# Spreading attention over the first MoE by the emitter's own clock instead of a table of unit times

## The chip, the cores and the metric

The kernel runs on one core of a Trainium2 chip. The metric is the device time of one execution in microseconds; before the change it is 749.09 us, the median of 3 runs (747.17 to 750.77). A profile was taken of one further execution.

## What is computed

Three layers, one after the other, all in float32 accuracy:

```python
scores = scale * q @ k.T          # 4 batches, 8 heads, 576 tokens, 64 wide
mask: block of 64 tokens sees itself and earlier blocks
x = softmax(scores) @ v           # then heads side by side: (4, 576, 512)

xk, xr = mixes of x[t] and x[t-1] by mu_k, mu_r        # first MoE
x = sigmoid(xr @ w_r) * (relu(xk @ w_k)**2 @ w_v)

h = gelu(x @ w_in); u, v = halves of h                  # second MoE
v = layernorm(v) * g_ln; v = w_sg @ v + b_sg            # over tokens
x = x + (u * v) @ w_out
```

The matmuls of the MoEs run on pairs: each operand is split into a rounded high part and the rest, and three products are summed (`xh*w0`, `xl*w0`, `xh*w1`). The weights come as float64 words and are put together on VectorE and ScalarE (`w_split`, lines 212 to 231).

## The kernel before

**Attention** is cut into 64 units: one head of one batch, and of its tokens the first 320 (kind LO) or the last 256 (kind HI). The list `units` runs LO of batch 0 (units 0 to 7), LO of batch 1 (8 to 15), HI of batch 0 (16 to 23), HI of batch 1 (24 to 31), and the same for batches 2 and 3 (32 to 63). A unit has three parts on PE: scores into the PSUM tiles `SA` and `SB` (`emit_S`; each tile has one buffer), transposes of the probabilities `P` into `T` (`emit_T`), and the products with V into `O` (`emit_PV`). Between them stand maxima (DVE, `stats`), exponentials (ACT, line 338), norms (DVE, line 348), copies of T (ACT `PH`, DVE `PL`), and after the products ACT `otmp` and DVE `xT`. The generator `attention` emits for step s, in this order: transposes of unit s-2, scores of unit s, products of unit s-2 (`LAG = 2`). The scores are so two units ahead of the products. Units below 16 (`DIRECT`) use plain float32 operands, with four passes in place of two in the emitter's count.

**The first MoE** runs in 8 halves of 288 tokens: (batch 0, first), (1, first), (0, second), (1, second), and the same of batches 2 and 3. A half is 240 matmuls of 288 columns: 96 with `w_k` (8 output blocks, 4 chunks of 3), 48 with `w_r`, 96 with `w_v`. It starts with `mix` (line 475), which makes `xh` and `xl` of the half in 4 chunks of two heads each: ACT `t`, DVE `t`, ACT `xh`, DVE or POOL `xl`. The last chunk needs the last head of the attention that this half reads, so half 1 needs units up to 15, half 2 up to 23, half 3 up to 31, half 4 up to 39, half 5 up to 47, half 6 up to 55 and half 7 all 64. The first two output blocks can do their chunks 0 to 2 without it (18 matmuls); the PSUM tile `M` has two buffers, so the 19th matmul is the first that must wait for the last chunk.

**Who sets the order.** `Order` (line 42) is a clock: `pe(ns)` adds what PE would need by `cost(n) = n / 2.4 + 13`, and work for the other engines is queued for a time on it. The loop at line 666 walks through `moe1()`, whose position x counts halves (x = 2.5 is the middle of half 2), and emits attention pieces while the attention time spent since unit 8, by the same `cost`, is below `target(x)`. `target` interpolates between knots: units needed at the next half, due at 0.85 of the half before it. It counts them with a table:

```python
UNIT_NS = [2000, 3120]                    # LO, HI
unit_t = [UNIT_NS[kind] for b, h, kind in units]
base = spent_a
```

At 0.85 of a half (line 674) whatever is still needed for the next half is emitted at once, without MoE between: `while done < need[i + 1]: att_piece()`. What is emitted so is then put in its final order on each engine by the compiler's scheduler. When all units are done, the attention memory is given back, the eight `w_in` tiles of the second MoE are loaded (line 209) and split.

Of the kernel before, what the change touches and what calls it, by code (L numbers as in the profile page):

```python
# [17 lines left out]
B, H, S = 4, 8, 576  # L18
# [2 lines left out]
CH0 = [0, 64, 192, 320, 448]  # L21
CHN = [64, 128, 128, 128, 128]
CHE = [64, 192, 320, 448, 576]

F64_MIN = struct.unpack("f", struct.pack("I", 896 << 20))[0]
F64_MAX = struct.unpack("f", struct.pack("I", (1151 << 20) - 1))[0]
# [15 lines left out]
class Order:  # L42
# [12 lines left out]
    def pe(self, ns):  # L55
        self.run(self.t)
        self.t += ns
# [12 lines left out]
    def run(self, t=float("inf")):  # L70
# [7 lines left out]
LO, HI = 0, 1  # L78
CHUNKS = [[0, 1, 2], [3, 4]]
# [3 lines left out]
GROUPS = [  # L83
    [
        ([(0, 0, 0), (0, 1, 64), (0, 2, 192)], 320),
        ([(1, 1, 0), (1, 2, 128), (2, 2, 256)], 384),
    ],
    [
        ([(0, 3, 0), (0, 4, 128)], 256),
        ([(1, 3, 0), (1, 4, 128), (2, 3, 256), (2, 4, 384)], 512),  # L90
        ([(3, 3, 0), (3, 4, 128), (4, 4, 256)], 384),
# [4 lines left out]
PRODS = [  # L96
    [(0, 0, 0, 0, 320), (1, 1, 0, 64, 256), (2, 1, 256, 192, 128)],
    [(0, 0, 0, 320, 256), (1, 1, 0, 320, 256), (2, 1, 256, 320, 256), (4, 2, 256, 448, 128),
     (3, 2, 0, 320, 256)],
]  # L100


DIRECT = 16
# [2 lines left out]
G = 2  # L106
X0_AT = 0.55
CONV2 = 2
UNIT_NS = [2000, 3120]


def cost(n):
    return n / 2.4 + 13
# [3 lines left out]
def fused_kernel(ctx: ExitStack, tc: tile.TileContext, first, qkv_lo, qkv_hi, mu,  # L117
# [6 lines left out]
    pe, at = order.pe, order.at  # L124
# [120 lines left out]
    units = [(b, h, kind) for p in range(0, B, 2) for kind in (LO, HI) for b in (p, p + 1) for h in range(H)]  # L245
    NU = len(units)
    loaded = set()
    raws, splits, vs, probs, trans, xt = {}, {}, {}, {}, {}, {}
# [34 lines left out]
    def split_v(n):  # L283
# [8 lines left out]
        copy(nc.scalar, V[:, 0:nj, odd, :], v)  # L292
        sub(nc.gpsimd, V[:, 0:nj, 1 - odd, :], v, V[:, 0:nj, odd, :].bitcast(F32))

    def emit_S(n):
        b, h, kind = units[n]
        order.need(("sp", n))
        Q, K, KL = splits.pop(n)
        chunks = CHUNKS[kind]
# [5 lines left out]
        if kind == HI:  # L305
            stc[4] = sb[:, 224:800]
        skc = [ka, ka, kb, ka, kb]
        P = probs[n] = pbuf[n % 2]
        pieces = {c: [(0, 288), (288, 576)] if c == 4 else [(0, CHE[c])] for c in chunks}
        pe(sum((2 if n >= DIRECT else 4) * cost(e - a) for c in chunks for a, e in pieces[c])  # L310
           + cost(64) * (n >= DIRECT) * sum(c > 0 for c in chunks))
        mx, sm = smax[n % 4], ssum[n % 4]
        t0, t1 = TOKENS[kind]
        nb = atile([128, 5], F32, "nb", 4)
        rr = atile([128, 5], F32, "rr", 4)
        for c in chunks:
            q0, m, e, st = CH0[c] - TOKENS[kind][0], CHN[c], CHE[c], stc[c]
            for k0, k1 in pieces[c]:
                o = st[0:m, k0:k1]
                if n < DIRECT:  # L320
                    mm(o, Q[:, q0:q0 + m], K[:, k0:k1], start=True, stop=True)
                    continue
                mm(o, Q[:, q0:q0 + m], K[:, k0:k1], start=True)
                if c > 0 and k1 == e:
                    mm(st[:, e - 64:e], mask_l, mask_r)
                mm(o, Q[:, q0:q0 + m], KL[:, k0:k1], stop=True)
# [14 lines left out]
        def norm():  # L341
# [3 lines left out]
            for c in chunks:  # L345
                m, e, o = CHN[c], CHE[c], POFF[c]

# [45 lines left out]
    def emit_PV(n):  # L393
        b, h, kind = units[n]
        order.need(("sv", n))
        V = vs.pop(n)
        odd = h % 2
        ot, ok = ptile("O", 512, 1)
        order.need(("PT", n))
        prods = PRODS[kind]  # L400
        pe(sum((2 if n >= DIRECT else 4) * cost(p[4]) for p in prods))
        t0, t1 = TOKENS[kind]
        for x, (j, u, src, q0, nq) in enumerate(prods):
            for i, part in enumerate(trans[n, u]):
                v = V[:, 64 * j:64 * j + 128] if n < DIRECT else V[:, j].rearrange("p a d -> p (a d)")
                mm(ot[:, q0 - t0:q0 - t0 + nq], v,
                   part[:, src:src + nq], start=x == 0 and i == 0, stop=x == len(prods) - 1 and i == len(trans[n, u]) - 1)
        for u in range(len(GROUPS[kind])):
            trans.pop((n, u))
        if (b, h // 2) not in xt:  # L410
            t = xt[b, h // 2] = mtile([128, S + 2], F32, "xT", XT_BUFS)
            nc.gpsimd.memset(t[:, 0:1], 0.0)
        t = xt[b, h // 2]
        r0, r1 = 64 * odd, 64 - 64 * odd
        tmp = atile([128, 320], F32, "otmp", 1)
        w = t1 - t0

        def ev1():
            copy(nc.scalar, tmp[r0:r0 + 64, 0:w], ot[r1:r1 + 64, 0:w])

        def ev2():
            nc.vector.tensor_tensor(out=t[r0:r0 + 64, 1 + t0:1 + t1], in0=ot[r0:r0 + 64, 0:w],  # L422
                                    in1=tmp[r0:r0 + 64, 0:w], op=ALU.add)

        def ev():
            copy(nc.scalar, t[r0:r0 + 64, 1 + t0:1 + t1], ot[0:64, 0:w])

        if n < DIRECT:
            at(0, ev, ok, ("x", b, kind))
            return  # L430
        at(0, ev1, ok)
        at(600, ev2, ok, ("x", b, kind))

    LAG = 2
# [176 lines left out]
    done, spent_a = 0, 0.0  # L611
# [29 lines left out]
    for i in range(1, len(halves)):  # L641
        if need[i] > knots[-1][1]:
            knots.append((i - 1 + MIX_AT, need[i]))
    unit_t = [UNIT_NS[kind] for b, h, kind in units]
    base = spent_a

    def cum(n):
        return sum(unit_t[H:n])

    all_t = cum(NU)  # L650

    def target(x):
# [316 lines left out]
```

## Time and profile before

| | |
|---|---|
| median of 3 runs | 749.09 us |
| the profiled execution, its own time | 752.42 us |
| its span, first to last instruction | 750.5 us |
| around the span | 1.9 us |
| mean granted TensorE clock | 0.973 of full speed |
| busy: PE, DVE, ACT, POOL | 93%, 71%, 58%, 44% |
| matmuls on PE | 4824 |

Stages along the span: attention alone with the first weights to 43 us, the first MoE with attention spread over it from 43 to 535 us, the second MoE from there. The view by stretches lists for each stretch the busy time of each engine, so idle time of PE is the stretch less its PE figure. The granted clock is 1.00 at 2.4 GHz and 0.50 at 1.2 GHz.

### The profile page before, as it was taken

How to read it: one execution, taken by the hardware profiler on the slowest of the kernel's cores; microseconds unless marked ns; L12 is line 12 of the kernel's file. 1: busy time of each engine (PE TensorE's matmuls, PEld its weight loads, DVE VectorE, ACT ScalarE, POOL GpSimd, SP SyncE). 2: the span in 40 equal slices, each digit the busy share in tenths (PEclk: the TensorE clock that was granted, in tenths of full speed). 3: DMA queues.
4: the chain of work that ended last, by engine and by line, in shares of the span. 5: the costliest groups of instructions: out<-in, count | busy, mean ns of one | idle time of the engine just before them, and what ended most of it. 6: DMA issues, size and time to landing. Idle time of an engine off the chain costs nothing.

```text
span 750.5 us, 13615 instructions
## 1 busy us (share of the span) xinstructions
PE 699.5 (93%) x4824; PEld 660.2 (88%) x4824; DVE 529.5 (71%) x1306; ACT 434.8 (58%) x1247; POOL 329.4 (44%) x381
## 2 busy tenths in 40 slices
PE   7878989998799899999899989988999999999998
PEld 5567869998799799999799979977999999999997
DVE  5999987778885766674885988479698736636323
ACT  4878768866795697794795788355361212122020
POOL 1437657834583386483584466134034204103021
PEclk9998999999999999999999999989999999999999
DMA  8571124223212222223222220062460120120101
GB/s 264 216 257 34 33 92 147 64 87 104 83 59 69 78 69 77 58 83 103 79 90 80 79 94 4 25 232 64 142 251 2 38 89 1 41 87 1 56 9 64
DMA packets 30724, 65.78 MB, mean 88 GB/s; under 512 B 5280, under 2 KB 16544, under 8 KB 30656
## 3 DMA queue, kind: packets, MB, share of 16 engines
q1 hardware_dynamic: 30512, 64.91, 26.5%
q8 instruction: 38, 0.62, 0.4%
q14 instruction: 30, 0.25, 0.1%
q10 hardware_dynamic: 144, 0.00, 0.0%
HBM read 55.47 MB, written 9.44 MB: 86 GB/s over the span
## 4 chain that ended last, share of the span: by engine, by line
PE 68%; DVE 14%; ACT 11%; DMA 3%; issue 3%; POOL 1%; SPq 0%; ACTq 0%; POOLq 0%; DVEq 0%
PE M L153 39%; PE O L153 14%; PE V L153 5%; PE T L370 5%; PE SB L153 3%; PE SA L153 3%; ACT P L338 2%; DVE u L222 2%; ACT PH L157 2%; DVE u L224 1%; DVE u L219 1%; DVE P L348 1%; DVE t L484 1%; DVE u L220 1%; DMA w<-w_k_dram 1%
## 5 line engine op out<-in xcount | busy, mean ns | idle before, releaser
L153 PE MATMUL M<-xh,w 128*128 128x288 f32 x768 | 178.8, 310 | 12.4 <-ACT xh L157 6.3
L153 PEld LDWEIGHTS M<-xh,w 128*128 128x128 f32 x768 | 133.0, 195 | 16.8 <-ACT R L535 7.9
L153 PE MATMUL M<-xl,w 128*128 128x288 f32 x384 | 117.2, 306 | 1.2 <-DVE xl L168 1.2
L153 PE MATMUL M<-kh,w 128*128 128x288 f32 x512 | 111.9, 300 | 3.7 <-ACT w L227 3.7
L168 DVE TENSOR_TENSOR PL<-T,PH 128x256 fp32r<-128x256 f32 (+3 forms) x128 | 68.9, 542 | 30.5 <-ACT PH L157 29.6
L153 PEld LDWEIGHTS M<-kh,w 128*128 128x128 f32 x512 | 84.7, 189 | 4.1 <-ACT w L227 4.1
L370 PE MATMUL T<-ident,P 128*128 128x128 f32 x480 | 83.5, 286 | 4.2 <-DVE P L348 2.4
L157 ACT ACTIVATE PH<-T 128x384 fp32r<-128x384 f32 (+4 forms) x144 | 68.0, 478 | 30.0 <-PE T L370 27.5
L168 POOL TENSOR_TENSOR KL<-qkv,K 128x576 fp32r<-128x576 f32 (+1 forms) x48 | 60.6, 1263 | 54.3 <-ACT K L157 40.8
L348 DVE TENSOR_SCALAR_CACHE_REDUCE P<-P,rr 64x64 f32<-64x64 f32 (+3 forms) x160 | 79.7, 536 | 1.1
L153 PEld LDWEIGHTS M<-xl,w 128*128 128x128 f32 x384 | 75.3, 196 | 2.2 <-DVE xl L168 1.8
L153 PE MATMUL M<-kl,w 128*128 128x288 f32 x256 | 76.0, 297 | 0.0
L847 POOL TENSOR_TENSOR gt<-gt,U 128x288 f32<-128x288 f32 x32 | 29.3, 920 | 100.5 <-DVE gt L843 100.4
L370 PEld LDWEIGHTS T<-ident,P 128*128 128x128 f32 x480 | 59.7, 147 | 9.1 <-issue 3.0
L168 POOL TENSOR_TENSOR xl<-t,xh 128x288 fp32r<-128x288 f32 x48 | 41.0, 855 | 49.3 <-ACT xh L157 46.8
L168 POOL TENSOR_TENSOR kl<-R,kh 128x288 fp32r<-128x288 f32 x64 | 57.8, 915 | 10.2 <-ACT kh L157 9.6
L168 POOL TENSOR_TENSOR w<-u,w 128x512 fp32r<-128x512 f32 x24 | 35.5, 1482 | 59.4 <-ACT w L227 59.4
L153 PE MATMUL O<-PH,V 128*128 128x256 f32 (+2 forms) x208 | 58.8, 294 | 3.0 <-DVE xT L422 3.0
L168 POOL TENSOR_TENSOR V<-qkv,V 128x320 fp32r<-128x320 f32 (+1 forms) x48 | 39.4, 820 | 45.2 <-ACT V L157 30.4
L153 PE MATMUL O<-PL,V 128*128 128x256 f32 (+2 forms) x208 | 56.3, 289 | 1.6 <-DVE PL L168 1.6
L153 PE MATMUL O<-gh,w 128*128 128x288 f32 x256 | 53.3, 294 | 0.0
L153 PE MATMUL M<-XHL,w 128*128 128x288 f32 x384 | 53.1, 295 | 0.0
(155 smaller groups left out, 1845.1 us busy)
## 6 DMA issues: line engine op xcount, KB each, us to landing
qkv<-qkv_hi_dram SPq DMA_DIRECT2D x32, 576.0 KB, 3.8
qkv<-qkv_lo_dram SPq DMA_DIRECT2D x16, 416.0 KB, 3.3
x2d<-x SPq DMA_DIRECT2D x32, 144.0 KB, 2.0
X<-x2d SPq DMA_DIRECT2D x4, 1152.0 KB
outT_dram<-o SPq DMA_DIRECT2D x32, 144.0 KB, 1.8
w<-w_k_dram SPq DMA_DIRECT2D x8, 512.0 KB
w<-w_v_dram SPq DMA_DIRECT2D x8, 512.0 KB, 7.6
w<-w_in_dram SPq DMA_DIRECT2D x8, 512.0 KB, 8.9
```

Of the source, the lines that this page charges most:

```text
L153: nc.tensor.matmul(out=out, lhsT=lhsT, rhs=rhs, start=start, stop=stop)
L157: nc.scalar.activation(out=out, in_=in_, func=AF.Copy)
L168: eng.tensor_tensor(out=out, in0=a, in1=b, op=ALU.subtract)
L219: nc.vector.tensor_scalar(out=v, in0=v, scalar1=F64_MIN, scalar2=F64_MAX, op0=ALU.max, op1=ALU.min)
L220: nc.vector.tensor_scalar(out=u, in0=u, scalar1=3, scalar2=0x3FFFFFFF, op0=ALU.logical_shift_left, op1=ALU.bitwise_and)
L222: nc.vector.scalar_tensor_tensor(out=u, in0=high, scalar=-0x40000000, in1=u, op0=ALU.bitwise_and, op1=ALU.bitwise_or)
L224: nc.vector.scalar_tensor_tensor(out=u, in0=low, scalar=29, in1=u, op0=ALU.logical_shift_right, op1=ALU.bitwise_or)
L338: nc.scalar.activation(out=P[0:m, po:po + e], in_=st[0:m, 0:e], func=AF.Exp, scale=0.125, bias=nb[0:m, c:c + 1], accum_out=sm[0:m, c, 0:1])
L348: nc.vector.tensor_scalar(out=P[0:m, o:o + e], in0=P[0:m, o:o + e], scalar1=rr[0:m, c:c + 1], scalar2=None, op0=ALU.mult, op1=ALU.add, acc ...
L370: nc.tensor.transpose(t[:, o:o + 128], P[:, POFF[c] + CH0[j]:POFF[c] + CH0[j] + 128], ident)
L484: nc.vector.scalar_tensor_tensor(out=t1, in0=x[:, s0 + 1:s0 + 1 + HF], scalar=mu_t[:, i, c:c + 1], in1=t1, op0=ALU.mult, op1=ALU.add)
L847: nc.gpsimd.tensor_tensor(out=gt, in0=gt, in1=U[b][:, m, fs], op=ALU.mult)
```

## The change

The table goes. `score_ns` and `out_ns` give what `emit_S`, `emit_T` and `emit_PV` hand to the clock, and the calls of `pe` in `emit_S` and `emit_PV` use them, with the same values as before. `cum(n)`, the attention time due when n units are done, sums these values: outputs of units 8 to n-1 and scores of units 8 to n+1. `base` is lowered by `cum(8)`.

```diff
--- before.py
+++ after.py
@@ -21,6 +21,7 @@
 CH0 = [0, 64, 192, 320, 448]
 CHN = [64, 128, 128, 128, 128]
 CHE = [64, 192, 320, 448, 576]
+PIECES = [[(0, 288), (288, 576)] if e == 576 else [(0, e)] for e in CHE]
 
 F64_MIN = struct.unpack("f", struct.pack("I", 896 << 20))[0]
 F64_MAX = struct.unpack("f", struct.pack("I", (1151 << 20) - 1))[0]
@@ -106,7 +107,6 @@
 G = 2
 X0_AT = 0.55
 CONV2 = 2
-UNIT_NS = [2000, 3120]
 
 
 def cost(n):
@@ -292,6 +292,15 @@
         copy(nc.scalar, V[:, 0:nj, odd, :], v)
         sub(nc.gpsimd, V[:, 0:nj, 1 - odd, :], v, V[:, 0:nj, odd, :].bitcast(F32))
 
+    def score_ns(n):
+        f, cs = (2, CHUNKS[units[n][2]]) if n >= DIRECT else (4, CHUNKS[LO])
+        return sum(f * cost(e - a) for c in cs for a, e in PIECES[c]) + cost(64) * (f == 2) * sum(c > 0 for c in cs)
+
+    def out_ns(n, trans=True):
+        kind = units[n][2]
+        return (sum((2 if n >= DIRECT else 4) * cost(p[4]) for p in PRODS[kind])
+                + trans * sum(len(g) * cost(230) for g, _ in GROUPS[kind]))
+
     def emit_S(n):
         b, h, kind = units[n]
         order.need(("sp", n))
@@ -306,16 +315,14 @@
             stc[4] = sb[:, 224:800]
         skc = [ka, ka, kb, ka, kb]
         P = probs[n] = pbuf[n % 2]
-        pieces = {c: [(0, 288), (288, 576)] if c == 4 else [(0, CHE[c])] for c in chunks}
-        pe(sum((2 if n >= DIRECT else 4) * cost(e - a) for c in chunks for a, e in pieces[c])
-           + cost(64) * (n >= DIRECT) * sum(c > 0 for c in chunks))
+        pe(score_ns(n))
         mx, sm = smax[n % 4], ssum[n % 4]
         t0, t1 = TOKENS[kind]
         nb = atile([128, 5], F32, "nb", 4)
         rr = atile([128, 5], F32, "rr", 4)
         for c in chunks:
             q0, m, e, st = CH0[c] - TOKENS[kind][0], CHN[c], CHE[c], stc[c]
-            for k0, k1 in pieces[c]:
+            for k0, k1 in PIECES[c]:
                 o = st[0:m, k0:k1]
                 if n < DIRECT:
                     mm(o, Q[:, q0:q0 + m], K[:, k0:k1], start=True, stop=True)
@@ -398,7 +405,7 @@
         ot, ok = ptile("O", 512, 1)
         order.need(("PT", n))
         prods = PRODS[kind]
-        pe(sum((2 if n >= DIRECT else 4) * cost(p[4]) for p in prods))
+        pe(out_ns(n, False))
         t0, t1 = TOKENS[kind]
         for x, (j, u, src, q0, nq) in enumerate(prods):
             for i, part in enumerate(trans[n, u]):
@@ -641,12 +648,12 @@
     for i in range(1, len(halves)):
         if need[i] > knots[-1][1]:
             knots.append((i - 1 + MIX_AT, need[i]))
-    unit_t = [UNIT_NS[kind] for b, h, kind in units]
-    base = spent_a
 
     def cum(n):
-        return sum(unit_t[H:n])
-
+
+        return sum(score_ns(u) for u in range(H, min(NU, n + LAG))) + sum(out_ns(u) for u in range(H, n))
+
+    base = spent_a - cum(H)
     all_t = cum(NU)
 
     def target(x):
```

By the code's own `cost`, an LO unit of the first 16 is 3098 ns (scores 1116, output 1982) where the table said 2000; a later LO unit is 1955 ns, a HI unit 3080 ns. The table also counted no scores of the two units ahead. By the table, then, attention falls short of what is due by a knot, the lack is carried from half to half, and the rest is emitted there in one piece: 9.3, 9.5, 8.6, 8.1, 8.5, 7.5 and 5.2 us of the emitter's clock at halves 0 to 6, and after each the next pieces come only when the target has caught up, some 0.2 to 0.5 of a half later. With the change these pieces are 0.2, 1.3, 1.4, 1.0, 0.9, 1.3 and 1.1 us, and attention is emitted from the start of each half to its end.

What the scheduler makes of it on PE, at three places. First, the start of half 5 in the kernel before: `xh_4974` is this half's input, `w_276` and `w_328` hold chunks 2 and 3 of `w_k`, `O_5196` is the output of unit 48.

```order
L153 MATMUL O_5196<-PL1_5143,V_4832 128x256
L153 MATMUL O_5196<-PH1_5142,V_4832 128x256
L153 MATMUL O_5196<-PL1_5143,V_4832 128x256
L153 MATMUL O_5196<-PH2_5158,V_4832 128x128
L370 MATMUL T_5233<-ident_60,P1_90 128x128
L153 MATMUL SA_5278<-K_4966,Q_4965 128x448
L153 MATMUL SA_5278<-mask_r_64,mask_l_63 128x64
L153 MATMUL SA_5278<-KL_4967,Q_4965 128x448
L370 MATMUL T_5233<-ident_60,P1_90 128x128
L153 MATMUL M_5044<-xh_4974,w_328 128x288
L153 MATMUL M_5060<-xh_4974,w_328 128x288
```

Behind these transposes and scores stands the first matmul with chunk 3 (`w_328`). Between the 18th MoE matmul and it stand the products of unit 47, most of those of 48, the transposes of 48 and the first of 49, and scores of units 49, 50 and 51, with no MoE between them. The products of unit 47, which chunk 3 needs, stand behind the 18th matmul too.

The same unit's products with the change (`O_4942` is the output of unit 47, `kh_4208` belongs to half 4):

```order
L153 MATMUL O_4942<-PL0_4897,V_4689 128x320
L153 MATMUL O_4942<-PH1_4903,V_4689 128x256
L377 MATMUL T_4953<-ident_60,P0_89 128x128 x2
L153 MATMUL O_4942<-PL1_4904,V_4689 128x256
L153 MATMUL O_4942<-PH1_4903,V_4689 128x128
L153 MATMUL O_4942<-PL1_4904,V_4689 128x128
L153 MATMUL M_5004<-kh_4208,w_856 128x288
L153 MATMUL M_5004<-kl_4209,w_856 128x288
L153 MATMUL M_5004<-kh_4208,w_856 128x288
L377 MATMUL T_5018<-ident_60,P0_89 128x128 x4
```

They have moved into half 4, to its 220th matmul of 240, so 20 matmuls of half 4 and the first 9 of half 5, with scores and transposes of the next units, stand between them and the first matmul that reads chunk 3.

The start of half 2 with the change (`O_2417` is the output of unit 23, the last that half 2 needs; `xh_2317` is its input):

```order
L153 MATMUL O_2417<-PL2_2375,V_2102 128x128
L153 MATMUL O_2417<-PH2_2374,V_2102 128x256
L153 MATMUL O_2417<-PL2_2375,V_2102 128x256
L377 MATMUL T_2463<-ident_60,P1_90 128x128 x4
L153 MATMUL SB_2498<-K_2310,Q_2309 128x288
L153 MATMUL SB_2498<-KL_2311,Q_2309 128x288
L153 MATMUL SB_2498<-K_2310,Q_2309 128x288
L153 MATMUL SB_2498<-mask_r_64,mask_l_63 128x64
L153 MATMUL SB_2498<-KL_2311,Q_2309 128x288
L153 MATMUL M_2432<-xh_2317,w_328 128x288
L153 MATMUL M_2471<-xh_2317,w_328 128x288
```

Here the products of unit 23 still stand behind the 18th matmul of half 2, with two score blocks between the 18th matmul and `w_328`; before, it was two score blocks in front and a third behind the 20th matmul. Elsewhere the last needed products stand, counted in the MoE matmuls of PE:

| needed by | before | with the change |
|---|---|---|
| half 1 | half 0, 192 | half 0, 190 |
| half 2 | half 2, 18 | half 2, 18 |
| half 3 | half 3, 18 | half 2, 229 |
| half 4 | half 3, 204 | half 3, 216 |
| half 5 | half 5, 18 | half 4, 219 |
| half 6 | half 6, 18 | half 5, 239 |
| half 7 | half 7, 18 | half 7, 9 |

In half 6 with the change one block of scores and most of the products of unit 56 still stand between the 18th matmul and the first with chunk 3. On DVE the order in half 0 is the same up to the last weight tile of `w_split`, but for a few instructions that change places with a neighbour, and in half 7 the splitting of `w_in` begins behind the same mix steps as before.

## Rows read from the trace of the kernel before

**Rows 1.** The page: busy time and share of the span of each engine, and of the 40 slices (18.8 us each) PE's busy tenths and the granted clock in tenths.

```profile
PE 699.5 (93%) x4824; PEld 660.2 (88%) x4824; DVE 529.5 (71%) x1306; ACT 434.8 (58%) x1247; POOL 329.4 (44%) x381
...
PE   7878989998799899999899989988999999999998
...
PEclk9998999999999999999999999989999999999999
```

**Rows 2.** Busy time in stretches (us from the span's start; busy us and instructions of PE, PEld, DVE, ACT, POOL; granted clock; DMA share and GB/s). The cuts are at matmuls counted in PE's timeline: half h of the first MoE is 240 matmuls `M<-xh`, `M<-xl`, `M<-kh` or `M<-kl`; halves 2, 3, 5, 6 and 7 begin at 171.6, 246.9, 357.9, 421.3 and 486.3, and their 25th matmul is at 202.2, 264.8, 376.9, 442.8 and 496.9.

```profile
60.00:111.50 51.50, 44.92 (x273) 39.78 (x273) 48.33 (x112) 39.39 (x117) 33.32 (x30) 0.93 0.15 46
111.50:171.60 60.10, 59.91 (x461) 59.41 (x460) 44.44 (x102) 45.68 (x131) 40.03 (x42) 1.00 0.33 107
171.60:202.20 30.60, 23.37 (x155) 21.89 (x154) 25.57 (x61) 20.85 (x61) 13.50 (x15) 0.89 0.28 87
202.20:246.90 44.70, 44.49 (x346) 43.93 (x345) 32.80 (x81) 33.66 (x100) 27.33 (x35) 1.00 0.20 62
246.90:264.80 17.90, 14.43 (x102) 13.01 (x100) 12.96 (x48) 13.46 (x46) 7.25 (x9) 0.93 0.27 81
264.80:308.50 43.70, 42.35 (x325) 41.60 (x325) 28.16 (x97) 34.64 (x116) 27.09 (x38) 0.99 0.26 79
308.50:357.90 49.40, 48.97 (x386) 48.55 (x384) 30.59 (x104) 37.09 (x122) 30.21 (x36) 1.00 0.25 79
357.90:376.90 19.00, 14.79 (x95) 13.49 (x94) 17.10 (x41) 14.98 (x43) 10.20 (x11) 0.91 0.31 102
376.90:421.30 44.40, 44.21 (x343) 43.80 (x342) 31.90 (x74) 31.37 (x93) 26.81 (x30) 1.00 0.21 66
421.30:442.80 21.50, 17.43 (x119) 16.03 (x117) 20.46 (x46) 17.47 (x51) 11.59 (x12) 0.93 0.31 99
442.80:486.30 43.50, 43.30 (x337) 42.98 (x337) 30.17 (x70) 29.80 (x85) 19.98 (x24) 1.00 0.10 33
486.30:496.90 10.60, 7.75 (x54) 7.15 (x52) 4.49 (x10) 4.39 (x10) 0.72 (x1) 0.87 0.56 173
496.90:519.00 22.10, 17.77 (x97) 15.90 (x96) 21.93 (x29) 14.92 (x37) 14.21 (x15) 0.83 0.49 168
```

**Rows 3.** The same columns, from the end of the half's 18th matmul to its 25th, of halves 2, 3, 5, 6 and 7 in this order.

```profile
181.10:202.20 21.10, 14.28 (x85) 13.04 (x84) 16.61 (x39) 15.43 (x46) 9.35 (x10) 0.84 0.28 85
250.50:264.80 14.30, 10.83 (x73) 9.41 (x71) 10.40 (x42) 10.27 (x35) 5.91 (x7) 0.91 0.28 87
361.10:376.90 15.80, 11.59 (x72) 10.32 (x71) 14.15 (x34) 12.82 (x36) 7.87 (x8) 0.89 0.34 113
426.80:442.80 16.00, 11.93 (x76) 10.57 (x74) 15.14 (x33) 13.58 (x40) 8.69 (x9) 0.90 0.29 89
490.30:496.90 6.60, 3.75 (x21) 3.15 (x20) 2.62 (x7) 3.03 (x7) 0.00 (x0) 0.80 0.63 202
```

**Rows 4.** PE's timeline after the 18th matmul of half 2: the first score matmul of three units in a row (start us, duration us, what it is, and in brackets the idle time before it and what ended it).

```profile
183.87 0.74 PE L153 MATMUL SA<-K,Q 128*128 128x448 f32 x1 [2.43 <-ACT P L338]
190.46 0.47 PE L153 MATMUL SA<-K,Q 128*128 128x448 f32 x1 [1.60 <-ACT P L338]
197.50 0.71 PE L153 MATMUL SA<-K,Q 128*128 128x448 f32 x1 [1.56 <-ACT P L338]
```

**Rows 5.** The timeline of all engines at the start of half 7: the last matmul of the last unit's output, and what follows it until PE goes on.

```profile
492.38 0.28 PE L153 MATMUL O<-PL,V 128*128 128x256 f32 x1
492.70 0.38 ACT L157 ACTIVATE otmp<-O 64x256 f32<-64x256 f32 x1 [1.29 <-PE O L153]
493.11 0.43 DVE L422 TENSOR_TENSOR xT<-O,otmp 64x256 f32<-64x256 f32 x1 [1.11 <-ACT otmp L157]
493.63 0.54 ACT L483 ACTIVATE t<-xT,um_t 128x288 f32<-128x288 f32 x1 [0.56 <-DVE xT L422]
494.20 0.52 DVE L484 SCALAR_TENSOR_TENSOR t<-xT,mu_t,t 128x288 f32<-128x288 f32 x1 [0.66 <-ACT t L483]
494.75 0.44 ACT L157 ACTIVATE xh<-t 128x288 fp32r<-128x288 f32 x1 [0.58 <-DVE t L484]
495.25 0.50 PEld L153 LDWEIGHTS M<-xh,w 128*128 128x128 f32 x2 [2.79 <-ACT xh L157]
```

**Rows 6.** Two stretches at the lower granted clock and one at the full clock that holds MoE matmuls alone (columns as in Rows 2).

```profile
371.10:374.50 3.40, 3.40 (x17) 3.40 (x18) 2.28 (x8) 3.24 (x10) 1.35 (x3) 0.54 0.09 8
439.30:442.70 3.40, 3.26 (x13) 3.12 (x14) 3.40 (x10) 3.40 (x11) 2.22 (x3) 0.55 0.23 59
407.00:410.40 3.40, 3.40 (x28) 3.40 (x27) 0.46 (x1) 0.00 (x0) 0.00 (x0) 1.00 0.63 213
```

**Rows 7.** Stretches in which attention and MoE are mixed (columns as in Rows 2): the 25th to the 145th matmul of half 6, and the fourth block of eight of halves 4 and 3.

```profile
442.80:469.60 26.80, 26.60 (x207) 26.30 (x207) 21.76 (x51) 23.29 (x69) 18.26 (x21) 1.00 0.11 36
...
324.60:331.00 6.40, 5.96 (x46) 5.58 (x45) 5.60 (x19) 6.35 (x23) 5.62 (x8) 1.00 0.32 91
276.30:283.20 6.90, 6.00 (x48) 5.77 (x46) 5.18 (x18) 6.83 (x23) 6.16 (x10) 1.00 0.18 62
```

**Rows 8.** Waits between 484 and 524 us (who waited for whom: us in total, times, longest), and one piece of the chain of waits at half 3 (start us, us, what).

```profile
ACT w L227 <- DVE u L224: 5.2, 4, 2.3
PE M L153 <- ACT R L535: 4.0, 4, 2.5
...
249.33 4.26 DMA qkv<-qkv_lo_dram
```

## The prediction

> **What bounds the kernel now.** I read the page first: PE is busy for 93% of the span, DVE for 71%, ACT for 58%, and PE's digits fall below 9 in a few slices only, mostly where the granted clock falls too [rows 1]. So the time is PE's work, plus the idle time of PE, plus what the lower clock costs. Next I cut the span at the halves of the first MoE [rows 2]. Idle PE is the stretch less its busy time, and it sits at the start of some halves: 30.60 - 23.37 = 7.2 us in half 2, 3.5 in half 3, 4.2 in half 5, 4.1 in half 6, 2.9 in half 7. Half 1, with the end of half 0 before it, lost 0.2 us in 60, and half 4 lost 0.4 in 49. The rest of halves 2, 5 and 6 lost 0.2 us each. Nearly all of the idle time at a start lies between the 18th and the 25th matmul: 6.8, 3.5, 4.2, 4.1 and 2.9 us [rows 3], and the granted clock there is 0.80 to 0.91.
>
> The order rows in the part on the change say what runs there: attention alone, three units in a row, since the last chunk of the half's input needs the last of them. Alone, units follow each other at 6.6 and 7.0 us (190.46 - 183.87 and 197.50 - 190.46), and each time PE waits 1.6 to 2.4 us for ACT's exponentials to free the score tile [rows 4]. This is latency: in the stretches of [rows 3] no engine is full throughout (DVE 79% in half 2, 73% in half 3). After the last unit comes the mix of the last chunk: PE finishes at 492.66, and five steps on ACT and DVE later it loads weights again at 495.25, 2.6 us in all with nothing in the way [rows 5].
>
> At 1.20 GHz, the lower level, 3.4 us hold 13 to 17 matmuls where 28 MoE matmuls fit at 2.40 GHz [rows 6]. The shapes differ, so I do not take the ratio but the half: 3.4 us of busy PE at half speed cost 1.7 us, less a little idle, 1.5 us. From half 1 to the start of half 7 the clock falls in those starts alone and is 0.99 or 1.00 in every other stretch [rows 2], so such spells follow waits.
>
> **The change, step by step.** Work on PE is the same: as many scores, transposes and products, none added. No DMA is added either; the loads of `qkv` move with their units and come at an even pace. In half 3 the chain ran through one of these loads for 4.26 us [rows 8], because three units in a row used up the three buffers; spread, that wait has no reason.
>
> Half 3 and half 5: the last needed products move from behind the 18th matmul to the 229th and 219th of the half before. In half 5, 20 matmuls and then 9 at 3.40 / 28 = 0.12 us each, with a unit's scores and products, some 5 us of PE, cover the 2.6 us of the mix chain, and also a chain twice as long under load. I take away all but 0.2 us: 3.3 + 4.0 = 7.3 us of waiting. Half 6: products at 239, so 19 matmuls (2.3 us), transposes and scores cover about 4 us, but a block of scores still stands in front of the last chunk. I leave 1.5 us of 4.1: 2.6 us gained. Half 7: the products move from 18 to 9, so 9 matmuls (1.1 us) cover part of the 2.6 us chain. I leave 1.4 of 2.9: 1.5 us gained. Half 2: the wait stays, with two units in a row in place of three. By that share 6.8 x 2/3 = 4.5 us stay: 2.3 us gained. Together 3.3 + 4.0 + 2.6 + 1.5 + 2.3 = 13.7 us.
>
> The clock: the spells of halves 3 and 5 and the second of the two in half 2 should go with their waits, that of half 6 in half of the cases: 3.5 x 1.5 = 5.2 us.
>
> What is added: attention now runs at the even rate of 8 units per 240 matmuls also where there was none. Nothing was hidden in those MoE-only stretches, since PE was full in them. The nearest stretch is the 25th to 145th matmul of half 6: 207 - 120 = 87 attention matmuls, a little over three units of 27, where the change asks for four. It has 0.2 us of idle PE in 26.8, with ACT at 87% and DVE at 81% [rows 7]; a fourth unit adds to PE as well as to them, so both stay near or under 90%. The worst pieces are two single blocks with ACT full: 0.4 us of 6.4 and 0.9 of 6.9 [rows 7]. The bounds for seven halves are thus 0 and 7 x 0.9 = 6.3 us, twice that if it happens twice in a half. I take 3.0 us, nearer to the long stretch.
>
> Half 0 I cost at nothing: DVE is busy for 48.33 of 51.50 us there [rows 2] with splitting weights, and its order hardly changes. If the extra attention delays the last weight tiles, it costs up to 2 us; if work fills the gap behind them, it gives as much. Half 7 after its 25th matmul is also left as it is: PE waits there for `R` on ACT (4.0 us), which stands behind weight copies that wait for DVE (5.2 us) [rows 8], and DVE is busy for 21.93 of 22.10 us [rows 2]. The splitting begins behind the same mix steps as before. The second MoE does not change.
>
> Sum: 13.7 + 5.2 - 3.0 = 15.9 us. The profiled execution took 752.42 us, so it would take 736.5. That execution is 3.3 us above the median of 749.09, and I subtract the same from the median: 733.2, forecast **733 us**. From the bounds: all waits of [rows 3] (21.4 us) and six spells (9.0) gone and nothing added gives 719; the added waits at 12.6 us in place of 3.0 give 743.
>
> **Rivals.** (1) *The wait moves with the units.* If DVE and ACT fall behind the even pace, the last needed unit is late at each start, as the order says for half 2. Halves 3, 5 and 6 would then keep two of three units in a row: of 3.5 + 4.2 + 4.1 only a third, 3.9, goes, with 2.3 in half 2, 1.5 in half 7 and two spells (3.0), less 3.0: 7.7 us, 741 us. For it: DVE and ACT are over 80% busy in the mixed stretch. Against: that stretch lost only 0.2 us.
>
> (2) *Slower: ACT becomes the bound in the first 96 matmuls of a half,* where MoE's own `R`, `kh` and mix already fill it (6.35 of 6.40 us, 6.83 of 6.90 [rows 7]). Before, part of each half's units came later, or alone. If PE lost 0.9 us in each 6.9 over such a stretch of 22 us, that is 2.9 us a half and 20 us in seven; against the gain of 18.9 and with a spell of low clock in each half (10.5 us), 749 + 20 - 18.9 + 10.5 = 761 us. It decides from 2.7 us a half on. Against: halves 1 and 4 before have attention from their first matmuls and lost 0.2 and 0.4 us in all.
>
> (3) *The low clock spreads.* One long wait becomes many short ones, and each half has a spell of low clock: 7 x 1.5 = 10.5 us off the gain, 744 us. Against: the two blocks with 0.4 and 0.9 us of waits kept a granted clock of 1.00 [rows 7]. The Trainium skill, "TensorE: Matmul & The Clock Gate", section "A second HAM failure mode: psum-queue depth-cycling", says that frequent small idle gaps between groups of matmuls can make the clock go back and forth between its two levels. By that rule this rival would hold; the trace so far does not agree with it at gaps of this size.
>
> (4) *The change does nothing on the chip*, because the scheduler had already evened things out, as in halves 1 and 4: 749 us. Against: for halves 3, 5 and 6 the final order differs.
>
> **How the numbers follow.** Forecast 0.67 (727 to 740), rival 1 0.17, rival 2 0.05, rival 3 0.05, rival 4 0.06. Half a per cent is 3.75 us, about what a measurement here can tell from no change, so faster means below 745.3 and slower above 752.8. Faster: 0.67 + 0.15 + 0.03 = 0.85; the same: 0.06 + 0.02 + 0.02 = 0.10; slower: 0.05. The range 723 to 745 takes in the forecast with most of its bounds, rival 1 and part of rival 3, about 8 in 10.
>
> **What would show it.** In the changed profile the granted clock is 1.00 over the starts of halves 3 and 5, and idle PE there is under 0.5 us; half 2 keeps a wait for the exponentials and one spell; half 7's start keeps the mix chain; idle PE in the mixed stretches stays under 0.5 us a half; and PE's busy time falls by about 5 us, by the clock alone. I am wrong if half 5 still waits on `xh`, if ACT is full over the first 96 matmuls with PE idle beside it, or if half 0 grows by more than 2 us.

## The result and the profile after

The changed kernel takes 718.62 us, the median of 4 runs (717.42 to 721.05), against 749.71 (747.17 to 750.77) of the kernel before: a ratio of 0.959, interval 0.956 to 0.963. It gains 31 us where 16 were forecast, and lies below the range of 723 to 745. The profiled execution took 721.05 us with a span of 719.1.

The page of the kernel after: engines, then PE's busy tenths and the granted clock in 40 slices; it answers to [rows 1].

```profile
PE 685.7 (95%) x4824; PEld 651.1 (91%) x4824; DVE 537.0 (75%) x1306; ACT 434.9 (60%) x1247; POOL 328.0 (46%) x381
...
PE   7888989999999999999999999869999999999998
...
PEclk9998999999999999999999999999999999999999
```

Idle PE is the span less its busy time: 719.1 - 685.7 = 33.4 us, where it was 750.5 - 699.5 = 51.0. So 17.6 us of waiting went. The same 4824 matmuls take 13.8 us less; the granted clock accounts for 11.6 of that (the table further down), and the rest is open. The two make the 31.4 us between the profiled executions.

The view by stretches of the kernel after, cut at the same matmuls as [rows 2] (start and end us, length, busy us and instructions of PE, PEld, DVE, ACT, POOL, granted clock, DMA share, GB/s). Half 1 begins at 122.5, half 2 at 179.0, half 3 at 243.0, half 5 at 345.0, half 6 at 404.5, half 7 at 460.0.

```profile
59.40:122.50 63.10, 56.69 (x352) 50.32 (x351) 57.30 (x132) 47.96 (x141) 45.07 (x40) 0.95 0.26 80
122.50:129.50 7.00, 7.00 (x56) 6.97 (x55) 6.97 (x16) 5.68 (x18) 3.00 (x4) 1.00 0.16 58
129.50:179.00 49.50, 49.50 (x385) 49.12 (x385) 40.82 (x95) 38.72 (x114) 31.14 (x35) 1.00 0.26 82
179.00:191.30 12.30, 11.00 (x86) 10.51 (x85) 11.66 (x28) 10.12 (x30) 5.81 (x6) 1.00 0.36 108
191.30:243.00 51.70, 51.21 (x401) 50.38 (x401) 41.98 (x109) 43.31 (x131) 31.67 (x41) 1.00 0.24 74
243.00:248.50 5.50, 5.50 (x46) 5.50 (x45) 4.55 (x16) 5.25 (x17) 3.37 (x5) 1.00 0.42 112
248.50:293.70 45.20, 45.15 (x359) 44.91 (x358) 35.46 (x116) 39.05 (x130) 28.48 (x41) 1.00 0.28 85
...
299.10:345.00 45.90, 45.90 (x361) 45.80 (x360) 36.21 (x107) 39.35 (x124) 30.99 (x36) 1.00 0.31 99
345.00:351.70 6.70, 6.70 (x55) 6.67 (x53) 6.63 (x16) 4.69 (x14) 2.33 (x3) 1.00 0.18 67
351.70:404.50 52.80, 52.44 (x402) 51.26 (x402) 45.68 (x100) 41.97 (x123) 33.90 (x36) 1.00 0.28 88
404.50:412.70 8.20, 7.49 (x59) 7.05 (x57) 7.85 (x20) 7.03 (x21) 4.98 (x5) 1.00 0.32 90
412.70:460.00 47.30, 46.77 (x363) 46.43 (x364) 33.83 (x76) 33.99 (x98) 22.95 (x27) 1.00 0.11 36
460.00:466.70 6.70, 4.97 (x36) 4.31 (x34) 2.40 (x6) 2.50 (x6) 0.00 (x0) 1.00 0.69 193
466.70:504.00 37.30, 30.88 (x214) 30.18 (x215) 35.61 (x51) 21.45 (x47) 15.50 (x16) 0.95 0.37 127
```

From half 1 to the 25th matmul of half 7 every stretch is at 1.00, and the long ones have next to no idle PE. The starts of halves 2, 3, 5 and 6 shrank from 30.6, 17.9, 19.0 and 21.5 us to 12.3, 5.5, 6.7 and 8.2; attention moved from them into the stretches behind, which grew.

The same columns from the end of the 18th matmul to the 25th, of halves 2, 3, 5, 6 and 7; they answer to [rows 3].

```profile
182.80:191.30 8.50, 7.20 (x56) 6.71 (x55) 7.96 (x21) 6.75 (x20) 3.85 (x4) 1.00 0.27 84
246.95:248.50 1.55, 1.55 (x15) 1.55 (x14) 1.55 (x4) 1.45 (x5) 0.94 (x3) 1.00 0.23 28
349.95:351.70 1.75, 1.75 (x17) 1.75 (x15) 1.75 (x5) 1.07 (x3) 0.88 (x1) 1.00 0.00 0
407.75:412.70 4.95, 4.24 (x33) 3.80 (x31) 4.68 (x14) 3.78 (x12) 2.09 (x3) 1.00 0.33 125
463.40:466.70 3.30, 1.57 (x9) 0.91 (x7) 1.52 (x4) 2.13 (x5) 0.00 (x0) 1.00 0.90 273
```

Halves 3 and 5 wait for nothing there, half 2 for 1.3 us, half 6 for 0.7 and half 7 for 1.7.

PE's timeline behind the 18th matmul of half 2, the rows that answer to [rows 4] (start us, duration us, in brackets the idle time before and what ended it).

```profile
182.94 0.37 PE L153 MATMUL SA<-K,Q 128*128 128x448 f32 x1
...
186.27 0.39 PE L153 MATMUL O<-PH,V 128*128 128x256 f32 x1 [0.79 <-DVE xT L429]
...
187.39 0.47 PE L153 MATMUL SA<-K,Q 128*128 128x448 f32 x1 [0.51 <-ACT P L345]
```

The two units follow each other at 187.39 - 182.94 = 4.45 us, where it was 6.6 and 7.0, and the wait for the exponentials is 0.51 us where it was 1.6 to 2.4.

The timeline of all engines at the start of half 7, three steps of the mix chain of [rows 5].

```profile
462.53 0.38 ACT L157 ACTIVATE otmp<-O 64x256 f32<-64x256 f32 x1 [3.45 <-PE O L153]
...
464.58 0.44 ACT L157 ACTIVATE xh<-t 128x288 fp32r<-128x288 f32 x1 [0.59 <-DVE t L491]
...
465.08 0.54 PE L153 MATMUL M<-xh,w 128*128 128x288 f32 x2 [1.39 <-ACT xh L157]
```

From `otmp` to PE it is 465.08 - 462.53 = 2.55 us, as before (495.25 - 492.70); the MoE matmuls now cover all but 1.39 us.

The trace shows one row of the order in the part on the change in another light. `O_2417` is the output of unit 24, not of unit 23: the transposes right behind it read `P1`, the buffer of odd units, so they are those of unit 25, and in the trace its products end at 189.2 us, 0.9 us before the 19th MoE matmul at 190.10, which is too short for the mix chain of 2.55 us. Unit 23's last product ends at 184.7, so all of unit 24's products and two blocks of scores stand between it and the 19th matmul. The counts in the table of that part are right.

### The profile page after: what moved, and what is told of

It reads as the page before. It is cut to its first block, busy times and chain, and to the rows that moved or that the text cites. A ratio compares the mean times of both kernels' runs of the same rounds, so it can differ in the third digit from the quotient of the medians.

```text
span 719.1 us, 13612 instructions
## 1 busy us (share of the span) xinstructions
PE 685.7 (95%) x4824; PEld 651.1 (91%) x4824; DVE 537.0 (75%) x1306; ACT 434.9 (60%) x1247; POOL 328.0 (46%) x381
## 4 chain that ended last, share of the span: by engine, by line
PE 69%; DVE 16%; DMA 8%; ACT 4%; issue 2%; SPq 0%; POOL 0%; ACTq 0%; DVEq 0%; POOLq 0%
PE M L153 40%; PE O L153 13%; PE T L377 5%; PE V L153 5%; PE SB L153 3%; PE SA L153 3%; DVE u L222 2%; DVE u L224 2%; DMA w<-w_k_dram 2%; DVE P L355 2%; DVE t L491 2%; DVE stats L338 1%; DMA xtr<-x2d 1%; DMA w<-w_v_dram 1%; ACT P L345 1%
## 5 line engine op out<-in xcount | busy, mean ns | idle before, releaser
L153 PE MATMUL M<-xh,w 128*128 128x288 f32 x768 | 176.2, 306 | 9.2 <-ACT R L542 7.8
L153 PEld LDWEIGHTS M<-xh,w 128*128 128x128 f32 x768 | 130.4, 192 | 11.6 <-ACT R L542 9.6
L153 PE MATMUL M<-kh,w 128*128 128x288 f32 x512 | 117.3, 302 | 1.2 <-POOL w L168 1.0
L153 PE MATMUL M<-xl,w 128*128 128x288 f32 x384 | 115.3, 301 | 0.3 <-DVE xl L168 0.3
L168 DVE TENSOR_TENSOR PL<-T,PH 128x256 fp32r<-128x256 f32 (+3 forms) x128 | 69.0, 543 | 20.0 <-ACT PH L157 18.8
L153 PEld LDWEIGHTS M<-xl,w 128*128 128x128 f32 x384 | 73.4, 191 | 1.1 <-DVE xl L168 0.8
L153 PE MATMUL O<-PH,V 128*128 128x256 f32 (+2 forms) x208 | 57.2, 284 | 0.9 <-DVE xT L429 0.8
L822 ACT ACTIVATE U<-M 128x288 f32<-128x288 f32 x32 | 13.1, 410 | 67.8 <-PE M L153 67.8
```

Of the source, the lines that this page charges most:

```text
L153: nc.tensor.matmul(out=out, lhsT=lhsT, rhs=rhs, start=start, stop=stop)
L168: eng.tensor_tensor(out=out, in0=a, in1=b, op=ALU.subtract)
L822: nc.scalar.activation(out=U[b][:, m, fs], in_=p, func=AF.Gelu_apprx_tanh)
```

## What was tried

The theory I went on with: the price is that of **blocks**. Where the last needed products stand behind the 18th matmul, attention runs alone there, PE waits for its units, and the clock falls; what matters is in which halves that happens, and not how good the numbers are that set the pace. Half 2 of the kernel after already shows that the place of the products alone does not set the price: they stand behind the 18th matmul as before, and it waits for 1.3 us at a clock of 1.00. Against it: the price goes with the lack at each half (half the lack, half the price); the exact unit times, or the two units of scores ahead, are what pays; the kernel pays for PE work and not for waits. Each expectation names the theories that it weighs in its own words. Ratios are to the kernel before, run beside each.

**Without the scores ahead**, from the kernel after:

```diff
-        return sum(score_ns(u) for u in range(H, min(NU, n + LAG))) + sum(out_ns(u) for u in range(H, n))
+        return sum(score_ns(u) + out_ns(u) for u in range(H, n))
-    base = spent_a - cum(H)
+    base = spent_a
```

> The changed kernel with the scores of the two units ahead left out of the sum again (each unit counted as its own scores and outputs, base not lowered). Theory A (what counts is how much attention is left to be emitted in one block at 0.85 of a half): the lack at the knots changes by 0.2 to 2 us, so 718 to 722 us, low-clock spells between 120 and 460 us at most one. Theory B (the scores ahead are what the change is about): most of the gain is lost, above 735 us.

721.19 us, ratio 0.961 (the kernel after: 0.959). The lead of the scores is worth 2.6 us by the medians and 1 by the ratios, within the spread. No block comes back.

**The table kept, with a constant head start**, from the kernel before:

```diff
-    base = spent_a
+    base = spent_a + 9900
```

> The kernel before the change, its table kept, with base raised by 9900 alone: attention gets a head start of the whole lack at the start of half 0 and is then due at the table's pace, so no block is left. Theory A: 716 to 723 us, at the level of the changed kernel, unless the head start in half 0, where DVE splits weights, costs more than 2 us. Theory B (true unit costs are needed): above 730 us.

722.03 us, ratio 0.964. With the wrong unit times of the table (2000 and 3120 ns) and one number added to the account, 27 of the 31 us are there. So the gain is not due to the right unit times.

**Half the lack, and the whole of it, put back** into the kernel after, whose unit times stay right:

```diff
-    base = spent_a - cum(H)
+    base = spent_a - cum(H) - 4500      # and, in a second kernel, - 9000
```

> The changed kernel with base lowered by a further 4500, so attention lags by 4.5 us of the emitter's clock in every half and about half of the old block is left at 0.85. Theory A with a price in proportion to the block: half of the 31 us comes back, 730 to 738 us. Theory C (short blocks wait, but do not bring the lower clock): 722 to 729 us, with 1 to 3 us of idle PE at the starts of halves 2, 3, 5, 6, 7 and at most two low-clock spells there. Theory B: 718 to 722 us.

> The changed kernel with base lowered by 9000: the blocks at 0.85 are as long as before the change, while the units are still counted at their true cost. Theory A: 744 to 752 us, idle PE of 3 to 7 us and a low-clock spell at the starts of halves 2, 3, 5 and 6. Theory B (the true costs matter, not the blocks): below 730 us.

With 4500: 741.51 us, ratio 0.987; with 9000: 745.86 us, ratio 0.995 (0.993 to 0.997). With the whole lack 26 of the 31 us are gone, and half the lack costs (0.987 - 0.959) / (0.995 - 0.959) = 0.78 of that; its 741.51 lies above every range that was given for it. The view by stretches of the kernel with 4500, the starts of halves 2, 3, 5 and 6:

```profile
172.10:193.40 21.30, 17.94 (x119) 16.27 (x118) 20.48 (x46) 17.29 (x50) 12.60 (x13) 0.92 0.30 93
239.30:256.90 17.60, 14.01 (x105) 12.21 (x103) 12.89 (x46) 13.23 (x46) 6.53 (x9) 1.00 0.29 82
350.20:365.00 14.80, 13.06 (x87) 12.44 (x86) 14.61 (x33) 12.38 (x38) 7.43 (x7) 0.88 0.40 130
410.80:430.20 19.40, 16.94 (x107) 15.89 (x106) 17.36 (x39) 14.62 (x41) 8.99 (x9) 0.82 0.23 72
```

The four starts are 73.1 us together, against 89.0 before [rows 2] and 32.7 after: blocks stand at all four again, with 11.2 us of idle PE and the clock down in three. But half the lack in the emitter did not make half a block on PE. Attention matmuls between the 18th and the 19th MoE matmul of halves 2, 3, 5 and 6, counted in the traces: 54, 44, 39 and 57 before the change, 57, 44, 35 and 54 with 4500, and 43, 0, 8 and 21 in the kernel after. So this run does not show what a shorter block costs. In its half 5 the last needed products stand behind the 9th matmul, ahead of the 18th, and it still has 1.7 us of idle PE and a clock of 0.88.

**One block put back**: at half 5 in full, at half 5 with half the lack, and at half 2. From the kernel after:

```diff
-        while done < NU and spent_a - base < target(x) and 4 * units[done][0] + units[done][1] // 2 < free_x:
+        while done < NU and spent_a - base < target(x) - 9000 * (3.85 < x < 4.85) and 4 * units[done][0] + units[done][1] // 2 < free_x:
# second kernel:                                      - 4500 * (3.85 < x < 4.85)
# third kernel:                                       - 9000 * (0.85 < x < 1.85)
```

> The changed kernel with the target lowered by 9000 in one half only (x from 3.85 to 4.85), so one block stands before half 5. Theory A: the price of one block by itself, 4 us of waiting and 1.5 us of clock at the start of half 5, so 723 to 726 us, and nothing elsewhere. If a block also delays the units after it, halves 6 and 7 show waits too and it costs 8 to 12 us. If single blocks are absorbed: 718 to 720 us.

> The changed kernel with the target lowered by 4500 for x from 3.85 to 4.85 only: a block of half the length before half 5. If the price follows the length, half of the 6.4 us of e5_late_h4: 721 to 722.5 us. If what counts is that the last needed products fall behind the 18th matmul of half 5, as they do here too, nearly the whole price: 723 to 726 us.

> The changed kernel with the target lowered by 9000 for x from 0.85 to 1.85 only, so one block stands before half 2, as e5_late_h4 has one before half 5. Theory A (each block has its own price, waits and the low clock behind them): 6 to 9 us more than the changed kernel, 725 to 728 us, with 4 us or more of idle PE and one or two low-clock spells at the start of half 2 and nothing new from half 3 on. If blocks only cost together: 718 to 720 us.

724.97 us (ratio 0.965), 726.02 (0.967) and 726.54 (0.968). By the ratios that is 4, 6 and 6 us for one block, with about 4 us of uncertainty each, and 6 to 8 us by the medians. Half the lack at half 5 is no test of a shorter block: in the traces of the first two kernels the instructions stand in the same order on PE, DVE, ACT and POOL (by operation, tile name and shape), so 0.965 and 0.967 are one kernel measured twice. In it the last needed products of half 5 fall behind the 18th matmul, and the lateness goes on into half 6, where the expectation for the first kernel had nothing. The start of half 5 with the whole lack, then those of halves 5 and 6 with half of it:

```profile
339.51:354.69 15.18, 12.67 (x78) 12.08 (x77) 12.97 (x29) 10.78 (x32) 7.43 (x7) 0.82 0.26 89
341.17:354.48 13.31, 10.76 (x80) 9.92 (x78) 11.72 (x27) 10.72 (x32) 6.60 (x7) 1.00 0.31 101
404.93:419.47 14.54, 12.77 (x88) 12.22 (x86) 12.49 (x30) 10.06 (x30) 5.40 (x6) 0.88 0.32 95
```

With half the lack idle PE is 2.6 + 1.8 us, where the kernel after has 0 and 0.7, and the clock takes 0.12 x 14.54 = 1.7 us: 5.4 us, near to what the ratio says (5.5). In the other execution of the same order the waits of half 5 are the same (1.43 and 1.09 us, here 1.42 and 1.09), but the clock fell there too, by 0.18 x 15.18 = 2.7 us, and the stretch is 1.9 us longer. The start of half 2 in the third kernel:

```profile
171.20:198.18 26.98, 23.55 (x152) 21.82 (x151) 24.59 (x59) 20.96 (x61) 13.41 (x14) 0.87 0.35 109
```

It is 27.0 us long again, with 3.4 us idle and 0.13 x 27.0 = 3.5 us lost to the clock; the kernel after had 1.3 and none.

**One block removed** from the kernel before:

```diff
-        while done < NU and spent_a - base < target(x) and 4 * units[done][0] + units[done][1] // 2 < free_x:
+        while done < NU and spent_a - base < target(x) + 10500 * (3.85 < x < 4.85) and 4 * units[done][0] + units[done][1] // 2 < free_x:
```

> The kernel before the change with the target raised by 10500 for x from 3.85 to 4.85 only: one of its blocks, that of half 5, is spread, the others stay. Theory A: the waits and the spell of half 5 go, 5 to 7 us, 743 to 746 us. If the even pace elsewhere is needed for it: 748 to 752 us.

742.67 us, ratio 0.988 (0.984 to 0.993): 8 us by the medians, 9 by the ratio, for one block. Its starts of halves 3, 5 and 6:

```profile
245.65:261.70 16.05, 13.10 (x100) 11.68 (x99) 11.72 (x44) 12.57 (x45) 6.51 (x9) 1.00 0.32 90
357.98:364.70 6.72, 6.72 (x56) 6.69 (x54) 5.59 (x15) 4.86 (x14) 3.09 (x4) 1.00 0.25 71
411.10:430.77 19.67, 17.61 (x115) 15.85 (x115) 18.51 (x44) 16.35 (x48) 11.32 (x11) 0.91 0.26 84
```

Half 5 lost its 4.2 us of waiting and its spell (0.09 x 19.0 = 1.7 us); half 6 still has its block, with 2.1 us of waiting in place of 4.1. Half 3 runs in the order of before, and this execution had no spell there: it is 1.9 us shorter than in [rows 2], with nothing changed there.

**The blocks filled with work that nobody needs**: in the kernel before, the transposes in the blocks ahead of halves 2 and 6 written three times (98 more) and, in a second kernel, twice (49 more). Each writes the same data to the same place again.

```diff
+    block = [False]
-        for j, c, o in tiles:
+        for j, c, o in tiles * (3 if block[0] else 1):
...
+            block[0] = i in (1, 5)
             while done < need[i + 1]:
                 att_piece()
+            block[0] = False
```

> The kernel before the change with each transpose of the two blocks before halves 2 and 6 written three times in place of once (same values, 98 transposes more, at 0.13 us each 13 us of PE work). If the blocks are bound by the chain through ACT and DVE and the low clock follows PE's idle time, most of the 13 us falls into the waits (11.3 us at these two starts) and spells go: 745 to 754 us. If the blocks are bound by PE's own work: 760 us or more.

> The kernel before, with the transposes of the blocks before halves 2 and 6 written twice (49 transposes more, about 6.5 us of PE work; written three times it was 98 and no difference in time). The order of the last needed products is that of before. Theory A (a block's length is set by its waits, and a spell at the lower clock is half covered by them): the filled blocks lose some of their idle time and of their spells, and the time stays within 3 us of before, 748 to 752. Theory B (each spell costs its full 1.5 us, three of them lie in these two blocks, and the added work hides in the idle time): the spells go and the time falls by 3 to 5 us, 746 or less. Theory C (the added work is paid in full): 756.

752.64 us with 98 more, ratio 1.001 (0.999 to 1.004), and 750.15 with 49 more, ratio 1.000 (0.998 to 1.003). The work costs little or nothing that these runs can tell. Where it went is another matter. Halves 1 and 2, and 5 and 6, to the 25th matmul; first the kernel before (its starts of halves 2 and 6 are in [rows 2]):

```profile
119.62:171.60 51.98, 51.79 (x401) 51.36 (x400) 40.23 (x95) 39.98 (x117) 32.53 (x35) 1.00 0.25 81
...
357.90:421.30 63.40, 59.00 (x435) 57.29 (x434) 49.00 (x113) 46.34 (x136) 37.01 (x40) 0.97 0.24 77
```

then the kernel with 98 more, all four stretches:

```profile
119.66:178.89 59.23, 59.04 (x464) 58.59 (x463) 45.80 (x107) 43.23 (x125) 34.18 (x38) 1.00 0.25 77
178.89:202.88 23.99, 19.11 (x150) 18.13 (x150) 20.31 (x49) 18.26 (x53) 11.05 (x12) 1.00 0.30 96
356.35:423.27 66.92, 62.53 (x470) 60.80 (x469) 51.10 (x120) 48.49 (x142) 39.34 (x42) 0.97 0.25 81
423.27:440.14 16.87, 15.23 (x115) 13.89 (x113) 14.56 (x36) 12.50 (x36) 6.88 (x7) 1.00 0.25 80
```

The first two are 83.2 us with 614 matmuls where it was 82.6 with 556, the other two 83.8 with 585 where it was 84.9 with 554. On balance the starts themselves took in none of the added work: they have 150 and 115 matmuls where it was 155 and 119. The scheduler put it into the stretches ahead of them, which have 63 and 35 matmuls more and grew by 7.3 and 3.5 us; the starts shrank by 6.6 and 4.6 us. Over all four stretches PE did some 9 us more of work at the full clock (busy time less what the clock took); idle PE fell from 15.9 to 11.1 us, and the clock's share from 6.8 to 2.0, since the spells in the starts of halves 2 and 6 (0.89 and 0.93) are gone. The work was thus paid for half by waiting and half by clock, and PE's own work alone does not set the length of a stretch and its block. That latency does is not shown: DVE was busy for 79, 73, 90 and 95% of the stretches of halves 2, 3, 5 and 6 in [rows 3], and no run separates the two. The second kernel did not bring the 746 or less that a full price of every spell would give with all added work hidden. It is no clean test, since its starts of halves 2 and 6 kept spells (0.93 and 0.88).

**Further ahead still**, and **the weights of the second MoE split at half the pace** in half 7, both from the kernel after:

```diff
-    base = spent_a - cum(H)
+    base = spent_a - cum(H) + 4000
# other kernel:
-CONV2 = 2
+CONV2 = 1
```

> The changed kernel with base raised by 4000, so attention runs 4 us of the emitter's clock ahead. Theory A: the small waits left at the starts of halves 5 and 6 (1.0 us) go, those of halves 2 and 7 stay by the order; 716 to 719 us. If attention ahead loads DVE in half 0 too much: 720 to 724 us.

> The changed kernel with CONV2 = 1: the eight tiles of w_in are split over twice as many steps of half 7. The waits of half 7 behind its 25th matmul (6.1 us of idle PE and one low-clock spell) are put down to this splitting on DVE and ACT; if so they shrink by 3 to 6 us and the time is 712 to 717 us, unless the second MoE then waits for w_in and gives it back (718 to 722 us).

725.08 us (ratio 0.967) and 719.39 (0.960). A further 4 us of lead costs 6 us instead of helping. In its trace half 2 has a block again, which the change had shortened:

```profile
183.00:194.30 11.30, 7.80 (x58) 6.82 (x56) 10.51 (x23) 8.66 (x26) 5.16 (x6) 1.00 0.36 105
```

That is 3.5 us of idle PE behind the 18th matmul, for 1.3 after, and halves 3 and 4 wait for 1.6 and 1.9 us more behind their starts. Between the spans, 724.7 and 719.1 us, 2.5 us are idle PE and 3.1 busy time; at the start of half 0 the clock was 0.70 over 22.2 us, for 0.90 over 17.9 after. Both ranges of its expectation were missed. Why the lead brings half 2 its block back is open. The other kernel is no test of the splitting: its instructions stand in the order of the kernel after on PE, DVE, ACT and POOL, so 719.39 is a second measurement of the changed kernel, and what the waits behind the start of half 7 hang on is not shown.

## Why the prediction was too small

The direction, the places and the reason were right: the waits sat where [rows 3] put them, they went where the last needed products went ahead of the 18th matmul, and no rival came (no ACT bound, no spread of the low clock, no move of the waits). Only "this is latency" was read too narrowly, from halves 2 and 3; in halves 5 and 6 DVE is busy for 90 and 95% of the stretches of [rows 3]. The sum was wrong in three of its terms. Idle time and clock (one less the granted clock, times the stretch) by the rows of before and after:

| term | forecast | measured |
|---|---|---|
| waits, half 3 | 3.3 | 3.5 |
| waits, half 5 | 4.0 | 4.2 |
| waits, half 6 | 2.6 | 4.1 - 0.7 = 3.4 |
| waits, half 7 | 1.5 | 2.8 - 1.7 = 1.1 |
| **waits, half 2** | 2.3 | 7.2 - 1.3 = 5.9 |
| **waits added, halves 1 to 6** | -3.0 | 2.6 - 1.4 = +1.2 |
| **clock, halves 1 to 7** | 5.2 | 9.7 - 0 = 9.7 |
| half 7 after its 25th matmul | 0 | idle -1.9, clock +1.9 |
| start, half 0, second MoE | 0 | +0.3 |
| sum | 15.9 | 29.3 of 31.4 |

The other 2.1 us are PE time that I can't assign. Half 7 after its 25th matmul is, before (the row after is above):

```profile
496.90:535.10 38.20, 33.64 (x216) 31.74 (x216) 35.67 (x51) 21.37 (x47) 14.75 (x16) 0.90 0.32 109
```

**Half 2** failed at the step "By that share 6.8 x 2/3 = 4.5 us stay"; 1.3 us stayed. I took the wait to go with the number of units in the block, and the trace shows that it does not. Before, the 6.8 us are 2.43 us ahead of the first scores, 1.60 ahead of the second, 1.22 for the mix chain ahead of the 19th MoE matmul and 1.56 ahead of the third scores [rows 4]. After, the first scores follow MoE matmuls without a wait, the second unit costs 0.79 and 0.51 us, unit 24's work covers the mix chain (before, it stood there too, and 1.22 us were left), and MoE goes on behind it. The low clock is not the reason for the long period: from 183.87 to 190.46 it was 0.76, but from 190.46 to 197.50, the longer one, 0.98. Why DVE and ACT answered sooner in the kernel after, no run shows.

**The clock** failed at "should go with their waits, that of half 6 in half of the cases", priced at 3.5 spells. All the spells from half 1 to half 7's 25th matmul went: by [rows 2], 3.4 us in half 2, 1.7 in half 3, 1.7 in half 5, 1.5 in half 6 and 1.4 in half 7. I kept one for half 2 and one for half 7 because a wait stayed; the waits that stayed at the starts, each under 1.5 us, left the clock at 1.00 in this execution. The 9.7 us are those of one execution of each kernel: in the run that took out the block of half 5, half 3 had the order of before and no spell.

**Added waits** failed at "I take 3.0 us, nearer to the long stretch". The bound of the long stretch was the answer: eight units in 240 matmuls leave PE idle for 1.4 us in six halves, less than the 2.6 of before. The single blocks with ACT full [rows 7] did not multiply; why, no run shows, since the rest of half 3 took in more matmuls (359 for 325) and waited for less (0.05 us for 1.35).

Each of the three was set to the cautious side, and the sum of them made the forecast. The text had the right number as a bound, "all waits of [rows 3] (21.4 us) and six spells (9.0) gone and nothing added gives 719", and the range left it out, although the three terms hang together: one cause, the block, carries wait, spell and the lateness of the next half. The runs that put back or took out one block show that, with 4 to 9 us each; all of them put back cost 26 of the 31. That the bound comes so near to 718.62 is luck: of its 21.4 us of waits only 18.1 went, and 1.2 us in the other stretches, a little more of clock and the unassigned 2.1 made up for it.

Rival 3 had a rule beside it, of the Trainium skill, "TensorE: Matmul & The Clock Gate", section "A second HAM failure mode: psum-queue depth-cycling", by which frequent small idle gaps let the clock swing. The trace of the kernel after does not agree: from 122.5 to 466.7 us it has 5.2 us of small waits, in halves 2, 3, 5, 6 and 7, and the granted clock is 1.00 in every stretch. One execution with a block at half 5 does in part: there two waits of 1.43 and 1.09 us came before a clock of 0.50 from 349.8 to 353.2 us.

What stays open is how much of a spell's lost clock the engine would have waited for anyway. The table counts both in full. Where the same instructions ran in the same order in two executions, at different clocks, the rows give it: 1.9 us of length for 2.7 us of lost clock at the start of half 5 (the two runs above), 1.9 for 1.3 at the start of half 3 ([rows 2] and the run without the block of half 5), but only 1.0 for 3.7 in the rest of half 0, where DVE splits weights; the kernel after, then its repeat with `CONV2 = 1`:

```profile
61.69:122.83 61.14, 54.73 (x343) 48.84 (x342) 55.37 (x126) 46.00 (x137) 43.49 (x39) 0.94 0.27 84
59.83:119.94 60.11, 52.18 (x343) 45.78 (x341) 55.99 (x126) 46.44 (x139) 43.07 (x39) 1.00 0.26 81
```

So in the blocks the full count is not far off, though these are single pairs.

## What to carry to other kernels

When a pace is set by a model of costs, look first at where the model's error collects: here it collected in front of four deadlines, and a block that was put back or taken out was worth 4 to 9 us. Price such a block as one thing, wait and clock together, and put its whole removal inside the range; a constant head start can be worth nearly as much as the right costs, and more of it can be worth less. And look at the order that an experiment gets before reading its time: twice here a change of the source left it as it was, and half the lack gave blocks of the same length.

## What the runs showed of the hardware

- In 50 runs of the kernel before, the mean granted clock lay between 0.966 and 0.983 and the time between 755.93 and 746.18 us, and they go together (correlation -0.77). The line of time by clock has 3.8 us for 0.01 of clock, that of clock by time 6.4, and 0.01 of 750 us is 7.5. So the scatter alone leaves the price open; by the pairs of executions above, a us of lost clock cost 0.3 us in half 0 and 0.7 and 1.5 us in two blocks.
- The length of the waits did not decide whether the clock fell. The block in [rows 4], with no wait over 2.43 us, lost 3.4 us to it. In one order of half 5, waits of 1.43 and 1.09 us left the start at 0.82 in one execution and, with 1.42 and 1.09, at 1.00 in another. With 98 more transposes the start of half 2 had waits of 2.05, 1.26 and 1.56 us and stayed at 1.00; in the kernel after, 0.79 and 0.51 us there, and 1.39 in half 7, did too.
- 98 more transposes, some 11 us of PE work by the stretches that took them in (7.3 us for 63), changed the time by a ratio of 1.001 (0.999 to 1.004): waits and low clock behind them fell by as much.
